# Feature columns in the order slot, sign, pair, head, and a new order list up to the second attention unit, in an adaLN block with linear attention

## The chip, the cores and the metric

The kernel runs on one core of a Trainium2 chip. The metric is the device time of one execution in microseconds; the time before is 408.78 us, the median of three runs (408.36 to 409.27).

## The reference

One transformer block on x of 2048 rows by 576, in bf16: conditioned layer norm, linear attention with 32 heads of width 18, conditioned layer norm, and a feed-forward layer of 4608 with ReLU.

```
mod = (silu(c) @ w_mod) in six rows: sa, ca, ga, sb, cb, gb
h   = layernorm(x) * (1 + ca) + sa
q, k, v = h @ wqkv, split in 32 heads of 18
pq, pk  = q @ w_phi[h], k @ w_phi[h]
phi(p)  = concat(softmax(p), softmax(-p))          # 36 features per head
kv  = phi(pk)^T @ v          z = sum of phi(pk) over the rows
o   = phi(pq) @ kv / (phi(pq) @ z + 1e-6)
x   = x + ga * (o @ wo)
h   = layernorm(x) * (1 + cb) + sb
out = x + gb * (relu(h @ w1) @ w2)
```

## The kernel before

**Tiling.** The 2048 rows are 16 tiles of 128 (a tile's index is `t`). The map `w_phi` and the norm's scale are folded into the key and query weights first (`F0`, `FA0`, `FB0`, `SC0` and others, L351 and L364), so one projection gives `pk` or `pq`. The first stage, to about 88 us, projects all keys and values and the first queries, makes the key features and sums the key-value product over all tiles (`KVa` to `KVc`, L636). Behind it the queries are taken in units of two tiles (unit 0 to 7): attention output, second norm, and the feed-forward layer of that unit.

**Features.** Heads are in 11 groups of `GH` = 3 (the last has 2). A head's 18 raw features are 9 slots `f` of 2 (pair `e`). A group's 108 columns (`DW`) in `phik` (keys) or `room` (queries) are ordered sign, slot, pair, head before: first 54 columns for the positive softmax, then 54 for the negative. Keys are evicted from PSUM into the first 54 columns and stay there as raw values; queries are evicted into `pq` on their own. In `softmax_parts`, `ext` builds the minimum and maximum over a head's features as a tree on VectorE (L474 to L479; steps `MN` and `MX` for the four tiles of a key block, `qMN` and `qMX` for a query unit). `less` writes minimum minus value into the negative half (L487, `LO`) and value minus maximum into the positive one (L489, `HI`). Then come the exponential on ScalarE (`EX`, L516), the sums, logarithm and exponential of the negative (`RC`, L539 and L541), and the scale on VectorE (`SC`, L547 for keys in one instruction, L551 for queries in two). Sums are made in one of two ways: on TensorE as nine matmuls with the identity, one a slot, added up in the PSUM tile `ps_sum` (`SU`, L523, and `SA`, which adds the pairs, L527), or on VectorE as one reduction a tile (`SD`, L534). Seven of the eight key pairs and the first query unit use TensorE; key tiles 12 and 13 and the other query units use VectorE.

**Order.** The kernel is recorded under a manual schedule: TensorE, VectorE, ScalarE and the DMA queue of SyncE each execute in the order in which the steps are written. Up to the second unit the steps stand in a string, `order`, one name a step; a name's letters choose the function, its numbers are arguments, and a last `.1` hands an eviction to the other engine: `KE`, `VE` and `QE` (evictions of keys, values and queries) go to ScalarE by default and to VectorE with it; `FA0`, `FB0` (fold evictions), `SC0`, `SC1` (scaling of weight rows) and `KVE` (key-value eviction) go to VectorE by default and to ScalarE with it. `K.t`, `V.t`, `Q.t` are projections of ten matmuls; their PSUM tiles come from a pool of three. `LS`, `RS`, `LX`, `LT` are the first norm and its transposing DMA. `qT` transposes the scaled query features by DMA into `ET`; `NU.j` and `NV.j` multiply them with the key-value product for unit 0 and unit 1 (L677). `HA.q` and `HB.q` are the two phases, by halves of TensorE's rows, of one of nine groups of the first feed-forward layer for unit 0 (L807), `RL` its ReLU, `Y` the second layer (L907). `LM`, `LW`, `W2`, `WOL` load weights, `RD` loads a gate row.

The sums on TensorE, and on VectorE:

```
for f in range(DH // 2):
    T_.matmul(ps, lhsT=ident[:], rhs=e[:, :, :, f * G2:(f + 1) * G2], start=(f == 0), stop=(f == DH // 2 - 1))
...
V.tensor_reduce(out=t["l", b][:, k * 22:(k + 1) * 22].rearrange("p (g s) h -> p g s h", s=2), op=ALU.add,
                axis=mybir.AxisListType.X, in_=E[:, j].rearrange("p g (s f h) -> p g s h f", s=2, h=GH))
```

Of the kernel before, what the change touches and what calls it, by code (L numbers as in the profile page):

```python
# [8 lines left out]
P = 128  # L9
# [34 lines left out]
def kernel(  # L44
# [23 lines left out]
    V, A_, G, T_ = nc.vector, nc.scalar, nc.gpsimd, nc.tensor  # L68
# [17 lines left out]
    def copy(eng, dst, src):  # L86
        if eng is A_:
            A_.activation(out=dst, in_=src, func=ACT.Copy)
        else:
            eng.tensor_copy(out=dst, in_=src)  # L90
# [6 lines left out]
    ident = const.tile([P, P], BF16, name="ident")  # L97
# [363 lines left out]
    PARTS = [(0, 5 * GF), (5 * GF, D - 5 * GF)]  # L461


    def softmax_parts(E, src, n, whole):

        ng = n * NG

        def slots(a, s=0):
            return a[:, :, :, s * GF:(s + 1) * GF].rearrange("p n g (f c) -> p (n g) f c", c=G2)

        def ext(op):
            src_, w = src.rearrange("p n g c -> p (n g) c"), 4 * G2
            a = work.tile([P, 4 * NG, w], BF16, name="tree", tag="tree", bufs=1)[:, 0:ng]
            V.tensor_tensor(out=a, in0=src_[:, :, 0:w], in1=src_[:, :, w:2 * w], op=op)  # L474
            for w in (2 * G2, G2):
                V.tensor_tensor(out=a[:, :, 0:w], in0=a[:, :, 0:w], in1=a[:, :, w:2 * w], op=op)  # L476
            V.tensor_tensor(out=a[:, :, 0:G2], in0=a[:, :, 0:G2], in1=src_[:, :, 8 * G2:9 * G2], op=op)
            r = work.tile([P, 4 * NG, 2, GH], BF16, name="root", tag="root", bufs=4)[:, 0:ng]
            V.tensor_tensor(out=r, in0=a[:, :, 0:GH].unsqueeze(2).to_broadcast([P, ng, 2, GH]),  # L479
                            in1=a[:, :, GH:G2].unsqueeze(2).to_broadcast([P, ng, 2, GH]), op=op)  # L480
            return r.rearrange("p a e h -> p a (e h)")

        def less(j, mn, mx):
            f = slots(src[:, j:j + 2])
            r = (mn if mx is None else mx)[:, j * NG:(j + 2) * NG].unsqueeze(2).to_broadcast([P, 2 * NG, DH // 2, G2])
            if mx is None:
                V.tensor_tensor(out=slots(E[:, j:j + 2], 1), in0=r, in1=f, op=ALU.subtract)  # L487
            else:
                V.tensor_tensor(out=slots(E[:, j:j + 2], 0), in0=f, in1=r, op=ALU.subtract)  # L489
# [28 lines left out]
        def sums_pe(j):  # L518

            ps = t["s", j] = aux_tile("ps_sum")[:, 0:2 * NG * 2 * G2].rearrange("p (a c) -> p a c", c=G2)  # L520
            e = E[:, j:j + 2].rearrange("p n g (s c) -> p (n g) s c", s=2)
            for f in range(DH // 2):
                T_.matmul(ps, lhsT=ident[:], rhs=e[:, :, :, f * G2:(f + 1) * G2], start=(f == 0), stop=(f == DH // 2 - 1))  # L523
# [6 lines left out]
        def sums(j):  # L530
            b, k = j // 2 * 2, j % 2
            if ("l", b) not in t:
                t["l", b] = work.tile([P, 4 * NG, GH], FP32, name="ln_s", tag="ln_s", bufs=2)
            V.tensor_reduce(out=t["l", b][:, k * 22:(k + 1) * 22].rearrange("p (g s) h -> p g s h", s=2), op=ALU.add,  # L534
                            axis=mybir.AxisListType.X, in_=E[:, j].rearrange("p g (s f h) -> p g s h f", s=2, h=GH))

        def recip(j):
            l = t["l", j]
# [2 lines left out]
            A_.activation(out=r[:], in_=l[:].unsqueeze(2).to_broadcast([P, 4 * NG, 2, GH]), func=ACT.Exp, scale=-1.0)  # L541

        def scale(j):
            r = t["r", j][:].rearrange("p a e h -> p a (e h)")
            if whole:
                e = E[:, j:j + 2].rearrange("p n g (s f c) -> p (n g s) f c", s=2, c=G2)
                V.tensor_tensor(out=e, in0=e, in1=r.unsqueeze(2).to_broadcast([P, 4 * NG, DH // 2, G2]), op=ALU.mult)  # L547
                return
            for s in range(2):
                e, q = slots(E[:, j:j + 2], s), r.rearrange("p (a s) c -> p a s c", s=2)[:, :, s]  # L550
                V.tensor_tensor(out=e, in0=e, in1=q.unsqueeze(2).to_broadcast([P, 2 * NG, DH // 2, G2]), op=ALU.mult)  # L551
# [25 lines left out]
    pss, pq_zero = {}, set()  # L577
# [5 lines left out]

    def features(dst, ps, eng):

        copy(eng, dst[:, 0:10, :].rearrange("p (a g) c -> p a g c", a=2),
             ps[:, :, 0:5 * GF].rearrange("p a (g c) -> p a g c", c=GF))
        copy(eng, dst[:, 10, :].rearrange("p (f h) -> p f h", h=GH)[:, :, 0:2],
             ps[:, 1, 5 * GF:5 * GF + 36].rearrange("p (f h) -> p f h", h=2))

    def keys_out(t, eng):
        features(phik_g(t // TPB)[:, t % TPB, :, 0:GF], pss["k", t], eng)

    def queries_out(t, eng):
# [24 lines left out]
    KVZ = const.tile([P, NG, GH * VH], BF16, name="KVZ")
# [361 lines left out]
    FB0.3.1 KE.6 SC0.3 KE.4 MN.1 RS.5 B0 BE0.1.1 V.7 LX.5 LM.0 BE0.0.1 LS.14 LM.1 HI.1 PM.3 Q.2 LT.10 VE.7 QE.2 RS.6
    Q.1 HI.0 K.8 QE.1 LT.11 Q.7 KE.8.1 MX.1 EX.0 QE.7 LS.15 Q.0 LX.6 Q.3 LO.3 QE.0 RS.7 SU.0 K.10 LT.9 QE.3.1 HI.3 K.11
    K.9 EX.1 KE.11 LO.2 WOL qMN.0 SA.0 LX.7 KE.10 KE.9 LT.12 SU.1 HI.2 EX.3 K.12 RW.1 RW.0 MN.2 SA.1 qMX.0 KE.12 LT.15
    SU.3 RWE.0.1 LT.14 K.15 RC.0 W1 qLO.0 K.14 RWE.1.1 LO.4 EX.2 KE.15 qHI.0 LT.13 Q.14 LO.5 MX.2 SA.3 KE.14 qEX.0
    QE.14 K.13 V.9 RC.1 HI.5 SU.2 HI.4 RC2.0 KE.13 MN.3 Q.4 LW.1.1 LO.7 VE.9 qEX.1 SA.2 V.8 EX.4 EX.5 QE.4.1 Q.13 MX.3
    V.6 VE.8 LO.6 SC.0 qSU.0 V.13 RC.2 SC.2 VE.6 qSA.0 RD.2 QE.13 Q.12 SU.5 RC.3 HI.6 VE.13 SC.3 qRC.0 V.10 EX.6 SU.4
    VE.10 SA.5 RC2.2 V.11 RC.5 QE.12 VE.11 qSC.0 V.12 SA.4 HI.7 EX.7 SC.1 SD.12 Q.8 V.15 RD.0 SD.13 SC.5 VE.12 VE.15
    SU.7 RC.4 SA.7 SC.4 RC.6 V.14 qT.0 QE.8 KVa LW.1.0 SC.6 VE.14 RC.7 KVb RC2.1 SC.7 LW.0.0 KVc Q.11 WS.1 KVE.0 LW.2.1
    KVE.1 LW.0.1 QE.11 WS.0 NU.1 Q.6 NU.0 NUE.1 OT.1 Q.10 NUE.0 qMN.1 OT.0 OTE.1 QE.6 OTE.0 MCE2 WO.1 QE.10 WOE.1 WO.0
    WOE.0 S2.1.1 R2.1 S2.0 R2.0 Q.15 X2.1 X2.0 Q.9 qLO.1 PN.1 PN.0 QE.15 PNE Q.5 QE.5 QE.9 qMX.1 qHI.1 qEX.3 HA.0 HA.1  # L990
    HA.2 qMN.2 HB.0 LW.2.0 P2 HB.1 qSD.3 qEX.2 HB.2 qSD.2 LW.3.1 qMX.2 LW.3.0 W2.0.0 W2.1.0 RL.0 W2.0.1 HA.3 RL.1 qRC.1
    RL.2 RD.1 HA.4 HB.3 HB.4 HA.5 RL.3 HA.6 W2.2.1 HB.5 RL.5 qSC.1 HB.6 W2.1.1 qT.1 NV.0 RL.6 Y.1.0.0 NVE.0 W2.2.0 OU.0
    NV.1 qHI.2 RL.4 Y.1.0.1 HA.7 qLO.2 NVE.1 qEX.4 qSD.4 qEX.5 HA.8 OU.1 WA.0 HB.7 WB.0 qSD.5 WPE.0 qRC.2 HB.8 RL.7
    WA.1 Y.1.1.0 qSC.2 WB.1 Y.1.1.1 WPE.1 RL.8 Y.1.0.2 S3.0 S3.1 Y.0.0.0 R3 X3 Y.1.1.2 YE.1.0 qT.2 NW.0 XT NWE.0
    Y.0.1.0 MD.0 Y.0.1.1 YE.1.1 Y.0.0.1 NW.1 OW.0 MD.4 Y.0.0.2 MD.3 NWE.1 Y.0.1.2 MD.2 YE.0.0 MD.1 OW.1 YE.0.1
    """
    for step in order.split():
        name, *at = step.split(".")
# [126 lines left out]
```

## Time and profile before

| | |
|---|---|
| median of 3 runs | 408.78 us (408.36 to 409.27) |
| profiled execution | 409.36 us, of which the span is 407.6 us |
| busy TensorE, VectorE, ScalarE | 399.2, 232.3, 181.7 us |
| granted TensorE clock | 1.00 |
| key-value product starts, its last matmul ends | 82.85, 87.92 us |
| numerator of the second unit (NV.0) starts | 114.51 us |

The span is one profiled execution from its first to its last instruction; what lies around it makes up the difference to that execution's own time. Times in rows of the trace count from the span's start. A row of the timeline has start, duration, engine, line and operation, then output and input, the shape, and how many instructions it groups; what stands in square brackets is idle time before it and who ended it. A row of the groups ends with busy time in us and the mean of one in ns.

### The profile page before, as it was taken

To read this page: it belongs to the slowest core of one execution; us is meant where nothing else is said; L and a number is where in the kernel's file an instruction comes from. 1 tells how busy PE (TensorE), PEld (TensorE's weight loads), DVE (VectorE), ACT (ScalarE), POOL (GpSimd) and SP (SyncE) were. 2 spreads that over 40 slices of the span, in tenths; PEclk is the share of its full clock that TensorE was granted. 3 is DMA by queue.
4 is the path that set the end of the run, shared out by engine and by line. 5 is a ranking of instruction groups with operands and counts; after the bars stand their busy time and mean duration, and the time that the engine had idled before them with its cause. 6 is when DMAs were issued, how large, how long until landed. Compare 5 with 4: busy or idle time off the path is not lost.

```text
span 407.6 us, 10671 instructions
## 1 busy us (share of the span) xinstructions
PE 399.2 (98%) x4572; PEld 298.3 (73%) x4572; DVE 232.3 (57%) x603; ACT 181.7 (45%) x337; POOL 19.4 (5%) x123
## 2 busy tenths in 40 slices
PE   6899999999999999999999999999999999999997
PEld 3777777797877888888888888655467774447776
DVE  6889999999766756685886579423202310000111
ACT  5899999938653065216422450144530005552000
POOL 8100000000000000000000000000000000000000
PEclk9999999999999999999999999999999999999999
DMA  8968950499973401423374216400040000000001
GB/s 235 290 109 214 210 128 17 75 262 370 279 180 72 95 3 34 89 60 58 70 98 83 38 21 129 71 2 1 2 66 16 14 31 2 0 2 2 14 18 29
DMA packets 71001, 35.53 MB, mean 87 GB/s; under 512 B 56673, under 2 KB 67434, under 8 KB 70954
## 3 DMA queue, kind: packets, MB, share of 16 engines
q1 hardware_dynamic: 70352, 34.83, 37.9%
q8 instruction: 36, 0.59, 0.6%
q10 hardware_dynamic: 602, 0.02, 0.1%
q14 instruction: 11, 0.09, 0.1%
HBM read 19.27 MB, written 2.37 MB: 53 GB/s over the span
## 4 chain that ended last, share of the span: by engine, by line
PE 89%; DVE 5%; DMA 2%; ACT 1%; issue 1%; SPq 0%; ACTq 0%
PE ps_y L907 35%; PE ps_h L807 31%; PE ps_v L457 5%; PE ps_k L457 5%; PE ps_wo L807 4%; PE ps_q L457 3%; PE ps_sum L523 2%; DMA kv_raw<-in_A_wqkv_dram 1%; PE ps_kv L636 1%; DMA ET<-room 1%; PE ps_num L677 1%; DVE ln_s L534 1%; DVE tree L476 1%; PE ps_bias L372 1%; DVE xn L239 0%
## 5 line engine op out<-in xcount | busy, mean ns | idle before, releaser
L907 PE MATMUL ps_y<-w_sb,H 128*128 128x288 bf16 x864 | 109.3, 286 | 0.0
L907 PEld LDWEIGHTS <-H 128*128 128x128 bf16 x864 | 82.9, 98 | 22.3 <-issue 2.0
L807 PE MATMUL ps_h<-hT2all,w1a 64*128 64x256 bf16 (+1 forms) x960 | 78.5, 305 | 0.0
L915 DVE TENSOR_TENSOR outt<-ps_y,row_gb 128x288 bf16<-128x288 f32 (+2 forms) x33 | 14.7, 445 | 103.0 <-PE ps_y L907 103.0
L807 PEld LDWEIGHTS <-w1a 64*128 64x128 bf16 x960 | 46.8, 94 | 22.0
L807 PE MATMUL ps_h<-hT2all,w1b 64*128 64x256 bf16 (+1 forms) x768 | 62.8, 305 | 0.0
L863 ACT ACTIVATE H<-ps_h 128x512 bf16<-128x512 f32 x36 | 21.5, 596 | 81.3 <-PE ps_h L807 81.3
L457 PEld LDWEIGHTS <-hT 128*128 128x128 bf16 x480 | 46.1, 97 | 12.2 <-issue 0.4
L890 ACT ACTIVATE H<-ps_h 128x1024 bf16<-128x1024 f32 x36 | 36.0, 1018 | 37.8 <-PE ps_h L807 37.8
L807 PEld LDWEIGHTS <-w1b 64*128 64x128 bf16 x768 | 37.4, 94 | 18.0
L724 DVE TENSOR_TENSOR x_sb<-x_sb,ps_wo 128x288 bf16<-128x288 bf16 x28 | 11.4, 450 | 42.4 <-PE ps_wo L807 42.4
L807 PE MATMUL ps_h<-hT2all,w1c 64*128 64x256 bf16 (+1 forms) x216 | 33.4, 305 | 0.0
L907 PE MATMUL ps_y<-w_sb,H1m 128*128 128x288 bf16 (+2 forms) x270 | 32.4, 273 | 0.0
L907 PEld LDWEIGHTS <-H1m 128*128 128x128 bf16 x270 | 24.5, 98 | 5.2
L516 ACT ACTIVATE room<-room 128x1188 bf16<-128x1188 bf16 x16 | 18.6, 1189 | 15.7 <-DVE room L489 13.9
L811 POOL MEMSET token<- 1x2 bf16 x86 | 8.2, 96 | 311.8 <-PE ps_h L807 291.6
L457 PE MATMUL ps_q<-wfold,hT 128*128 128x270 bf16 (+1 forms) x160 | 21.6, 285 | 0.0
L457 PE MATMUL ps_v<-wv_sb,hT 128*128 128x288 bf16 x160 | 21.4, 286 | 0.1
L457 PE MATMUL ps_k<-wfold,hT 128*128 128x270 bf16 (+1 forms) x160 | 21.2, 285 | 0.0
L227 DVE BATCH_NORM_STATS2 bst<-x_sb 128x6 f32<-128x288 bf16 x46 | 18.6, 445 | 1.5 <-DMA x_sb<-in_A_x_dram 1.5
L534 DVE TENSOR_REDUCE ln_s<-room 128x66 f32<-128x1188 bf16 x14 | 18.7, 1368 | 0.0
L864 ACT ACTIVATE H1m<-ps_h 128x512 bf16<-128x512 f32 x30 | 17.8, 592 | 0.0
(156 smaller groups left out, 442.9 us busy)
## 6 DMA issues: line engine op xcount, KB each, us to landing
w_sb<-in_B_w_dram SPq DMA_DIRECT2D x6, 864.0 KB, 12.4
out_dram<-outt SPq DMA_DIRECT2D x15, 144.0 KB, 1.9
w1b<-in_B_w_dram SPq DMA_DIRECT2D x2, 1024.0 KB
x_sb<-in_A_x_dram SPq DMA_DIRECT2D x3, 576.0 KB, 10.3
w1a<-in_B_w_dram SPq DMA_DIRECT2D x2, 768.0 KB
kv_raw<-in_A_wqkv_dram SPq DMA_DIRECT2D x4, 288.0 KB, 5.0
wma<-in_w_mod_dram SPq DMA_DIRECT2D x2, 576.0 KB
wmb<-in_w_mod_dram SPq DMA_DIRECT2D x2, 576.0 KB
```

Of the source, the lines that this page charges most:

```text
L227: V.bn_stats(out=st[:, half, :], in_=x_sb[:, t0 + j, half * 288:(half + 1) * 288])
L457: T_.matmul(ps[:, 0:cn], lhsT=lhs[:, ci, :], rhs=w[:, ci, cs:cs + cn], start=(ci == 0), stop=(ci == KC - 1))
L516: A_.activation(out=E[:, j:j + k], in_=E[:, j:j + k], func=ACT.Exp)
L534: V.tensor_reduce(out=t["l", b][:, k * 22:(k + 1) * 22].rearrange("p (g s) h -> p g s h", s=2), op=ALU.add, axis=mybir.AxisListType.X, in_ ...
L724: V.tensor_tensor(out=xs[:, cs:cs + cn], in0=xs[:, cs:cs + cn], in1=p[:, 0:cn], op=ALU.add)
L807: i = T_.matmul(ps, lhsT=l, rhs=r, start=(phase == 0 and k < 2), stop=(phase == 1 and k >= len(items) - 2))
L811: g = last[key] = G.memset(token[:], 0.0)
L863: A_.activation(out=p2t["H1"].rearrange("p (e j) n -> p e j n", e=2)[:, :, i, :], in_=f1[i][:, :, 0:U * P], func=ACT.Relu)
L864: A_.activation(out=h1_more(i), in_=f1[i][:, :, U * P:], func=ACT.Relu)
L890: A_.activation(out=p2t["H1"].rearrange("p (e j) n -> p e j n", e=2)[:, :, 2 * q:2 * q + 2], in_=f1[q][:].rearrange("p e (h n) -> p e h n" ...
L907: T_.matmul(ps[:, 0, 0:cn], lhsT=h, rhs=p2t["w2"][:, k, c], start=(k == 0), stop=(k == NJ - 1))
L915: V.tensor_tensor(out=o[:, c], in0=ps[:, 0, 0:cn], in1=rows["gb"][:, c], op=ALU.mult)
```

## The change

A group's columns are now ordered slot, sign, pair, head: for each slot the six positive features, then the six negative ones. The raw keys therefore lie in runs of 6 with a step of 12, the keys' evictions write 90 such runs (the last group 9x2x2), and trees and subtractions read and write them so; queries still come from `pq`, which is contiguous. The matmul of a slot reads its 12 columns of a group as one run. A tile's sums on VectorE become two reductions, one a sign, over two axes. The queries' scale becomes one instruction like the keys'. `pad_keys` clears all columns of the last group.

```diff
@@ softmax_parts
+        def signs(a):
+            return a.rearrange("p n g (f c) -> p (n g) f c", c=2 * G2)
+        def raw(j, k):
+            return signs(E[:, j:j + k])[:, :, :, 0:G2] if src is None else src[:, j:j + k].rearrange("p n g (f c) -> p (n g) f c", c=G2)
@@ ext
-            V.tensor_tensor(out=a, in0=src_[:, :, 0:w], in1=src_[:, :, w:2 * w], op=op)
+            V.tensor_tensor(out=a.rearrange("p a (f c) -> p a f c", c=G2), in0=x[:, :, 0:4], in1=x[:, :, 4:8], op=op)
@@ less
-                V.tensor_tensor(out=slots(E[:, j:j + 2], 1), in0=r, in1=f, op=ALU.subtract)
+                V.tensor_tensor(out=e[:, :, :, G2:], in0=r, in1=f, op=ALU.subtract)
@@ sums_pe
-            e = E[:, j:j + 2].rearrange("p n g (s c) -> p (n g) s c", s=2)
+            e = signs(E[:, j:j + 2])
-                T_.matmul(ps, lhsT=ident[:], rhs=e[:, :, :, f * G2:(f + 1) * G2], start=(f == 0), stop=(f == DH // 2 - 1))
+                T_.matmul(ps.rearrange("p (a s) c -> p a (s c)", s=2), lhsT=ident[:], rhs=e[:, :, f], start=(f == 0), stop=(f == DH // 2 - 1))
@@ sums
-            V.tensor_reduce(out=t["l", b][:, k * 22:(k + 1) * 22].rearrange("p (g s) h -> p g s h", s=2), op=ALU.add,
-                            axis=mybir.AxisListType.X, in_=E[:, j].rearrange("p g (s f h) -> p g s h f", s=2, h=GH))
+            l = t["l", b][:, k * 22:(k + 1) * 22].rearrange("p (g s) h -> p g s h", s=2)
+            e = E[:, j].rearrange("p g (f s e h) -> p g s h f e", s=2, e=2, h=GH)
+            for s in range(2):
+                V.tensor_reduce(out=l[:, :, s], op=ALU.add, axis=mybir.AxisListType.XY, in_=e[:, :, s])
@@ scale
-            for s in range(2):
-                e, q = slots(E[:, j:j + 2], s), r.rearrange("p (a s) c -> p a s c", s=2)[:, :, s]
-                V.tensor_tensor(out=e, in0=e, in1=q.unsqueeze(2).to_broadcast([P, 2 * NG, DH // 2, G2]), op=ALU.mult)
+            e, r = signs(E[:, j:j + 2]), t["r", j][:].rearrange("p (a s) e h -> p a (s e h)", s=2)
+            V.tensor_tensor(out=e, in0=e, in1=r.unsqueeze(2).to_broadcast([P, 2 * NG, DH // 2, 2 * G2]), op=ALU.mult)
@@ keys_out
-        features(phik_g(t // TPB)[:, t % TPB, :, 0:GF], pss["k", t], eng)
+        e = phik_g(t // TPB)[:, t % TPB].rearrange("p g (f c) -> p (g f) c", c=2 * G2)
+        features(e[:, :, 0:G2], pss["k", t], eng)
@@ order, its line around the product
-    SU.7 RC.4 SA.7 SC.4 RC.6 V.14 qT.0 QE.8 KVa LW.1.0 SC.6 VE.14 RC.7 KVb RC2.1 SC.7 LW.0.0 KVc Q.11 WS.1 KVE.0 LW.2.1
+    SU.7 SD.12 SC.3 VE.13 SA.7 RC.6 Q.10 VE.14 SC.6 RC.7 KVa SC.7 QE.10 KVb RD.0 KVc WS.0 KVE.0 KVE.1.1 Q.13 NU.1 WS.1
...
```

The string `order` is rewritten from its first value projection to the end of unit 0. Of the evictions, VectorE now has values 1, 2, 5 and 15 (before: 2), keys 0 (before: 0, 1, 8) and, ahead of the product, no query (before: 3 and 4); the fold evictions FA0.1, FB0.0 and FB0.3 and the scaling SC0.4 move to it, while SC1.1, SC0.2 and KVE.1 move to ScalarE. One more phase of the feed-forward layer, HA.7, stands ahead of NV.0. The tree of unit 2's maximum (qMX.2) stands behind NV.0, its first subtraction (qLO.2) ahead of the scale qSC.1; the load W2.0.1 is fifth of the second weights, not third, and RD.1 is earlier.

ScalarE, the last instructions up to the last exponential of the keys (`phik_449` is the last block of four tiles, `v` are evicted values), before:

```order
L541 ACTIVATE rsum<-ln_s 128x264
L516 ACTIVATE phik_449<-phik_449 128x2376
L88 ACTIVATE v_95<-ps_v 128x32x18
L539 ACTIVATE ln_s<-ln_s 128x132
L541 ACTIVATE rsum<-ln_s 128x264
L88 ACTIVATE room<-ps_q 128x540
L88 ACTIVATE room<-ps_q 128x18x2
L88 ACTIVATE v_95<-ps_v 128x32x18
L516 ACTIVATE phik_449<-phik_449 128x2376
```

And now:

```order
L88 ACTIVATE room<-ps_q 128x540
L88 ACTIVATE room<-ps_q 128x18x2
L544 ACTIVATE ln_s<-ln_s 128x132
L546 ACTIVATE rsum<-ln_s 128x264
L544 ACTIVATE ln_s<-ln_s 128x132
L546 ACTIVATE rsum<-ln_s 128x264
L88 ACTIVATE v_96<-ps_v 128x32x18
L88 ACTIVATE v_95<-ps_v 128x32x18
L519 ACTIVATE phik_449<-phik_449 128x2376
```

Two pairs of logarithm and reciprocal and two values now stand between the last query eviction and the exponential, where there was one value.

VectorE, from the last subtraction of the keys to the last scale, before:

```order
L489 TENSOR_TENSOR phik_449<-phik_449,root 128x22x54
L547 TENSOR_TENSOR phik_446<-phik_446,rsum 128x2376
L534 TENSOR_REDUCE ln_s<-phik_449 128x66 x2
L547 TENSOR_TENSOR phik_448<-phik_448,rsum 128x2376
L527 TENSOR_REDUCE ln_s<-ps_sum 128x132
L547 TENSOR_TENSOR phik_448<-phik_448,rsum 128x2376
L547 TENSOR_TENSOR phik_449<-phik_449,rsum 128x2376 x2
```

And now:

```order
L492 TENSOR_TENSOR phik_449<-phik_449,root 128x198x6
L550 TENSOR_TENSOR phik_448<-phik_448,rsum 128x2376 x2
L540 TENSOR_REDUCE ln_s<-phik_449 128x11x3 x4
L550 TENSOR_TENSOR phik_447<-phik_447,rsum 128x2376
L530 TENSOR_REDUCE ln_s<-ps_sum 128x132
L550 TENSOR_TENSOR phik_449<-phik_449,rsum 128x2376 x2
```

Five scales stand there as before, but two come ahead of the reductions, of which there are four and not two.

TensorE at the numerator of the second unit (`ET` the transposed queries, `w1b` and `w1c` parts of the first feed-forward weights), before:

```order
L807 LDWEIGHTS w1b_1938
L807 MATMUL ps_h_2095<-hT2all_172,w1b_1938 128x256
L677 LDWEIGHTS ET_2154
L677 MATMUL ps_num_2157<-KVZ_174,ET_2154 128x57
L677 LDWEIGHTS ET_2154
```

And now, at the same count of instructions from the start:

```order
L806 LDWEIGHTS w1b_1840
L806 MATMUL ps_h_2074<-hT2all_172,w1b_1840 128x256
L806 LDWEIGHTS w1c_1192
L806 MATMUL ps_h_2153<-hT2all_172,w1c_1192 128x256
L806 LDWEIGHTS w1c_1192
```

The numerator has moved behind the twenty matmuls of HA.7, which begin here.

More of the change, by code (lines that the diff above doesn't have):

```diff
@@ L483, in less @@
         def less(j, mn, mx):
-            f = slots(src[:, j:j + 2])
+            f, e = raw(j, 2), signs(E[:, j:j + 2])
             r = (mn if mx is None else mx)[:, j * NG:(j + 2) * NG].unsqueeze(2).to_broadcast([P, 2 * NG, DH // 2, G2])
             if mx is None:
-                V.tensor_tensor(out=slots(E[:, j:j + 2], 1), in0=r, in1=f, op=ALU.subtract)
+                V.tensor_tensor(out=e[:, :, :, G2:], in0=r, in1=f, op=ALU.subtract)
             else:
-                V.tensor_tensor(out=slots(E[:, j:j + 2], 0), in0=f, in1=r, op=ALU.subtract)
+                V.tensor_tensor(out=e[:, :, :, 0:G2], in0=f, in1=r, op=ALU.subtract)
         t = {}
@@ L598, in queries_out @@
             G.memset(pq[b][:, :, NG - 1, :], 0.0)
-        features(pq[b][:, j], pss["q", t], eng)
+        features(pq[b][:, j].rearrange("p g (f c) -> p (g f) c", c=G2), pss["q", t], eng)
     def values_out(t, eng):
@@ L981 @@
[L981 to L985, printed above, removed]
@@ new lines @@
+    VE.0 K.2 LS.7 K.1 RS.2 LS.12 VE.2.1 LX.2 LQ.2 LQ.3 K.0 KE.2 LS.10 F0.4 RS.3 LT.4 LX.3 KE.1 KE.0.1 K.3 F0.0 FB0.4
+    LT.6 FA0.4 LS.11 LT.5 F0.1 LS.9 FB0.1 LT.7 KE.3 LS.13 FA0.1 V.4 FB0.0 MN.0 VE.4 FA0.0.1 K.6 LM.1 RS.6 SC0.4 F0.2
+    RS.4 LO.0 FB0.2.1 K.5 FA0.2.1 KE.6 V.7 LM.2 LX.4 MX.0 KE.5 SC0.0 SC0.2.1 F0.3 VE.7 PM.3 K.4 FA0.3.1 RS.5 FB0.3 KE.4
+    V.5 LS.14 HI.0 VE.5.1 K.7 KE.7 LT.8 PM.2 B0 SC0.1 LM.0 LX.5 LT.11 BE0.1.1 BE0.0.1 RW.1 SC0.3 LO.1 MX.1 LS.15 Q.0
+    HI.1 MN.1 RWE.1.1 RS.7 LX.6 Q.2 QE.2 QE.0 K.8 LO.3 Q.1 LO.2 LT.9 KE.8 K.9 Q.3 LT.10 EX.1 QE.1 EX.0 LX.7 SU.1 qMX.0
@@ new lines @@
+    HI.3 K.10 KE.9 qMN.0 KE.10 SU.0 HI.2 K.11 RW.0 LT.15 LT.14 QE.3 qLO.0 RC2.0 LT.13 EX.3 SA.0 SA.1 Q.7 RWE.0.1 KE.11
+    EX.2 RD.2 QE.7 K.15 Q.4 LT.12 SU.2 qHI.0 MN.2 K.13 KE.15 RC.0 MX.2 RC.1 QE.4 LO.5 LO.4 V.11 KE.13 VE.11 qEX.1 WOL
+    qEX.0 RD.1 K.14 SA.2 K.12 KE.12 SC.0 V.9 SU.3 KE.14 W1 RC.2 SC.1 LW.1.0 qSU.0 Q.14 HI.4 V.15 HI.5 RC2.2 VE.9 MN.3
+    qSA.0 LO.6 SA.3 EX.4 MX.3 SU.4 VE.15.1 EX.5 QE.14 Q.8 qRC.0 SU.5 RC2.1 V.10 HI.6 qSC.0 SC.2 QE.8 LW.0.1 Q.12 V.8
+    RC.3 SA.5 EX.6 SA.4 VE.10 qT.0 QE.12 RC.4 V.12 V.6 RC.5 VE.12 VE.8 V.14 LO.7 HI.7 SC.4 SC.5 V.13 EX.7 VE.6 SD.13
```

47 lines of the change are left out of this document (17 added, 30 removed).

## The prediction

> **What bounds the kernel now.** I read the first part of the page, then the busy time of the first stage, then the order of work at the two places where the order list changes what waits. The page, each engine's busy time and share of the span:
>
> ```profile
> PE 399.2 (98%) x4572; PEld 298.3 (73%) x4572; DVE 232.3 (57%) x603; ACT 181.7 (45%) x337; POOL 19.4 (5%) x123
> ```
>
> TensorE has work for 98% of the span, so only two things shorten the run: matmuls that take less time, and waits of TensorE that go. But the average hides the first stage, up to the key-value product. Its busy time in stretches, columns TensorE matmul, weight load, VectorE, ScalarE, GpSimd:
>
> ```profile
> 17.00:80.00 63.00, 62.93 (x565) 48.85 (x561) 59.80 (x139) 59.97 (x129) 2.56 (x11) 1.00 0.63 121
> 17.00:87.00 70.00, 69.93 (x732) 55.20 (x728) 66.80 (x145) 64.15 (x139) 2.56 (x11) 1.00 0.67 134
> ```
>
> There three engines are full: VectorE 66.8 of 70 us, ScalarE 59.97 of the 63 us up to the last exponential of the keys (3.03 us idle). Whoever makes TensorE faster here meets the other two. The end of that stage, in order of start:
>
> ```profile
> 77.78 2.19 ACT L516 ACTIVATE phik<-phik 128x2376 bf16<-128x2376 bf16 x1
> 80.43 1.35 PE L523 MATMUL ps_sum<-phik,ident 128*128 128x264 bf16 x9
> 82.85 5.23 PE L636 MATMUL ps_kv<-v,phik 128*128 128x57 bf16 x176
> 82.87 4.00 DVE L547 TENSOR_TENSOR phik<-phik,rsum 128x2376 bf16<-128x2376 bf16 x3
> 87.92 0.87 PE L457 MATMUL ps_q<-wfold,hT 128*128 128x270 bf16 x6
> ```
>
> The last exponential (EX.7) ends at 79.97; its sums on TensorE (SU.7) start at 80.43, so they have 0.46 us in hand. The last scale ends at 86.87; its two tiles are the last of sixteen in the product, which reaches them at about 82.85 + 14/16 x 5.07 = 87.29: 0.42 us in hand.
>
> **Sums on TensorE.** They stay 72 matmuls of 264 columns in 8 groups; what changes is that their operand is read in 22 runs of 24 bytes, not 44 of 12. Starts before, first V projections of 288 contiguous columns and what follows, then a group for keys and what follows, then the query group with rows that begin at its second, third, fourth and fifth matmul:
>
> ```profile
> 17.79 5.08 PE L457 MATMUL ps_v<-wv_sb,hT 128*128 128x288 bf16 x40
> 22.70 0.51 PE L457 MATMUL ps_k<-wfold,hT 128*128 128x270 bf16 x3
> 46.09 1.35 PE L523 MATMUL ps_sum<-phik,ident 128*128 128x264 bf16 x9
> 47.27 0.39 PE L457 MATMUL ps_k<-wfold,hT 128*128 128x270 bf16 x2
> 68.22 1.41 PE L523 MATMUL ps_sum<-room,ident 128*128 128x264 bf16 x9
> 68.36 0.47 PE L523 MATMUL ps_sum<-room,ident 128*128 128x264 bf16 x2
> 68.51 0.43 PE L523 MATMUL ps_sum<-room,ident 128*128 128x264 bf16 x2
> 68.66 0.42 PE L523 MATMUL ps_sum<-room,ident 128*128 128x264 bf16 x2
> 68.77 0.46 PE L523 MATMUL ps_sum<-room,ident 128*128 128x264 bf16 x2
> 69.47 0.29 PE L457 MATMUL ps_v<-wv_sb,hT 128*128 128x288 bf16 x1
> ```
>
> Contiguous: (22.70 - 17.79)/40 = 122.8 ns for 288 columns, so 112.5 for 264. Keys: (47.27 - 46.09)/9 = 131 ns. Query group: 1.25/9 = 139, and the matmuls of one group differ, 140, 150, 150 and 110 ns, though only the place of their runs differs. With the old layout's addresses, a slot's 12-byte runs touch 66 or 88 stretches of 16 bytes in the slow ones and 44 in the quick ones; the new runs start at a multiple of 8 bytes and touch 44 always. I take 114 to 116 ns: 63 x 16 + 9 x 24 = 1.2 us of TensorE time. Bounds: nothing (the cost is not of the runs) and 63 x 18.5 + 9 x 26.5 = 1.4. The Trainium skill, "Advanced Engine Details and Errata", section "SBUF Cachelines", says that lines are 16 bytes and that a line wants at least two hits; that fits the 110 against 150 ns above. Its "TensorE: Matmul & The Clock Gate", section "Wait — 56ns, not 53.3ns?", gives start to start as columns by 2.4 GHz plus about 2.5 ns, whatever the layout: by that the groups would already run at 112.5 and this term would be nothing; the rows disagree.
>
> All of it lies before the product, so SU.7 could start 1.1 us earlier, at 79.3, if its exponential were there. It had 0.46 us in hand, so ScalarE decides.
>
> **ScalarE up to the last exponential.** Counting both lists up to it, it gets 2 key evictions, 2 query evictions, 1 pair of logarithm and reciprocal and 1 scaling of a weight row more; 3 value evictions and 3 fold evictions fewer.
>
> ```profile
> L88 ACT ACTIVATE v<-ps_v 128x576 bf16<-128x576 f32 x15 | 9.6, 647 | 0.2
> L88 ACT ACTIVATE phik<-ps_k 128x540 bf16<-128x540 f32 x13 | 7.9, 616 | 0.0
> L88 ACT ACTIVATE phik<-ps_k 128x36 bf16<-128x36 f32 x13 | 2.7, 208 | 0.0
> L88 ACT ACTIVATE room<-ps_fold 128x432 bf16<-128x432 f32 x5 | 2.6, 530 | 0.7 <-PE ps_fold L351 0.7
> L88 ACT ACTIVATE room<-ps_fold 128x144 bf16<-128x144 f32 x6 | 1.6, 293 | 0.0
> L539 ACT ACTIVATE ln_s<-ln_s 128x132 f32<-128x132 f32 x16 | 5.0, 314 | 25.5 <-DVE ln_s L534 24.9 <-DVE ln_s L527 0.6
> L541 ACT ACTIVATE rsum<-ln_s 128x264 bf16<-128x264 f32 x16 | 6.8, 423 | 0.8 <-DVE phik L547 0.3
> ```
>
> 4 x (0.616 + 0.208) + 0.737 + about 0.5 - 3 x 0.647 - 0.530 - 2 x 0.293 = +1.5 us, against 3.03 us idle. With the idle unchanged the exponential would end at 81.5, with none at 78.4. Walking the new list by hand (each instruction starts at the later of its input and its predecessor, durations from such rows) I come to 80.0 to 80.1, with half of the idle used up. TensorE meanwhile waits for evictions and folds in six places, 0.04 to 0.2 us each, about as much as before. So SU.7 starts at 80.05, 0.38 earlier than before; its own group is 0.15 shorter, and one projection follows it as before (now a query's, not the last value's). The product starts and ends 0.5 us earlier, near 87.4. **Term one: -0.5 us**; 0.7 of the 1.2 us turns into waits. That the keys' evictions write 90 runs of 6 rather than 10 of 54 I cost at nothing: in these rows an eviction's price goes with its elements, 616 ns for 540 and 530 for 432; bound 0.1 us for each of 15, which would move the exponential by up to 1 us.
>
> **VectorE up to the last scale.** Its rows:
>
> ```profile
> L90 DVE CAST v<-ps_v 128x576 bf16<-128x576 f32 x1 | 0.8, 750 | 0.0
> L90 DVE CAST phik<-ps_k 128x540 bf16<-128x540 f32 x3 | 2.1, 711 | 0.1
> L90 DVE CAST phik<-ps_k 128x36 bf16<-128x36 f32 x3 | 0.6, 188 | 0.0
> L534 DVE TENSOR_REDUCE ln_s<-phik 128x66 f32<-128x1188 bf16 x2 | 2.7, 1380 | 0.0
> L527 DVE TENSOR_REDUCE ln_s<-ps_sum 128x132 f32<-128x264 f32 x8 | 3.4, 424 | 0.0
> L551 DVE TENSOR_TENSOR room<-room,rsum 128x1188 bf16<-128x1188 bf16 x16 | 11.7, 772 | 0.3
> L547 DVE TENSOR_TENSOR phik<-phik,rsum 128x2376 bf16<-128x2376 bf16 x8 | 10.8, 1386 | 0.0
> L489 DVE TENSOR_TENSOR phik<-phik,root 128x1188 bf16<-128x1188 bf16 x8 | 6.0, 770 | 0.0
> L474 DVE TENSOR_TENSOR tree<-phik 128x1056 bf16<-128x1056 bf16 x8 | 5.6, 700 | 0.1
> ```
>
> - Evictions: +3 values, -2 keys, -2 queries: 2.25 - 1.80 - 1.80 = -1.3; three fold evictions (one large, two small, at the ScalarE rows or a little more) +1.2, a scaling of a weight row away, -0.3.
> - Sums as two instructions: from 264 to 1188 elements a reduction grows from 424 to 1380 ns, 1.03 ns an element plus 0.15 fixed, so two of 594 cost 1.53 and not 1.38: +0.15 each, +0.3 for the two of the keys. The 14 for queries lie in stages where VectorE has slack.
> - Query scale as one instruction: 1.386 for 2 x 0.772: -0.16.
> - First step of the trees and both subtractions, strided now: nothing. The subtractions already work on 6-element runs by a broadcast operand at 0.65 ns an element (770 for 1188), and the first tree step, whole rows, has 0.66 (700 for 1056): contiguous or not, the same. Bound: one element at a time as the reduction, 1.03 + fixed.
>
> Sum -0.3 to about +0.15, since neighbours overlap. The last scale then ends near 86.6, and the product, 0.5 earlier, needs it at 86.8. It just fits; this is the next to be late.
>
> **Behind the product.** Half the key-value eviction goes to ScalarE as five small activations, about 5 x 0.21 = 1.05 us (the 36-element row), beside a query projection of 1.23 us: hidden, and TensorE needs it only for the ninth to eleventh group. The gap at NV.0, the numerator of the second unit, before:
>
> ```profile
> 109.94 3.95 SPq L664 DMA_TRANSPOSE ET<-room  x2
> 110.19 0.27 PE L807 MATMUL ps_h<-hT2all,w1c 64*128 64x256 bf16 x2
> 111.28 0.27 PE L807 MATMUL ps_h<-hT2all,w1c 64*128 64x256 bf16 x2
> 111.94 2.35 PE L807 MATMUL ps_h<-hT2all,w1b 64*128 64x256 bf16 x40
> 114.51 0.41 PE L677 MATMUL ps_num<-KVZ,ET 108*128 108x57 bf16 x8 [0.23 <-DMA ET<-room]
> ```
>
> Twenty matmuls of a first phase take 111.28 - 110.19 = 1.09 us, so the 40 end their turn at 111.94 + 2.18 = 114.12, and the numerator starts at 114.51: 0.39 us lost to the transposes. With one more phase ahead of it (HA.7), it is due at 114.12 + 1.09 - 0.5 = 114.7, when the transposes have landed even if they are no earlier. **Term two: -0.4 us.** Nothing else takes the place: the phase is only moved, and the fifth load of the second weights, now W2.0.1, has more than 2 us in hand as I follow the queue.
>
> Sum: -0.9 us. The profiled execution is 409.36 (span 407.6), so 408.46; the median of the runs is 0.58 lower than that execution: 407.9.
>
> **Rivals.**
> 1. The whole saving comes through: ScalarE finishes the exponential by 79.3, and some early waits (0.04 to 0.2 each) go as well. For it: 3.03 us of idle against 1.5 of new work. Against: the idle is made by what ScalarE waits for. -1.2 - 0.4 - 0.2 = -1.8: 407.0.
> 2. ScalarE eats everything: the exponential 0.4 us later than I walked, at 80.4 or after. For it: +1.5 us of work on an engine that is 95% full. -0.4 or nothing in all: 408.4 to 408.8.
> 3. The sums don't get quicker (the change doesn't do what it says): 131 ns stays. SU.7 then has as much in hand as before, and only NV.0 gains: 408.4. The clock page's rule above comes to the same time by the other road, that they are quick already.
> 4. The other side: the strided key features cost the trees their rate. Eight first tree steps at 1.03 ns an element, 1.24 for 0.70 us, are +4.3 us on VectorE, which has 0.2 in hand before the last scale; the product, 0.5 early, then ends 3.6 late, and term two takes 0.4 off: 412.0. It decides from 0.05 us a step. Against it the rows of 770 and 700 ns. The Trainium skill, "VectorE: DVE Perf Modes", section "Mode 2×_1P — pack two bf16 into one 32-bit read", asks for step ±1 and 4-byte alignment; runs of 6 keep both inside a run, and here only a run can show whether the jump between runs counts.
> 5. An early wait of the new order that I mis-walked (a value eviction on VectorE holding one of the three PSUM buffers) costs 1 us or more before the product: 409 to 410.
>
> **How the numbers follow.** A difference under 0.2%, 0.82 us, is about what a measurement of this kernel can't tell from none. Chances: my forecast 0.42 (407.4 to 408.4), rival 1 0.22, rival 2 0.12, rival 3 0.10, rival 4 0.07, rival 5 0.07. The forecast lies just past the bound (407.96), so 0.25 of its 0.42 count as faster, with 0.21 of rival 1 and 0.03 of rivals 2 and 3: 0.49. Same: 0.17 + 0.01 + 0.19 = 0.37. Slower: rivals 4 and 5, 0.14. The range leaves out rival 4 and the tails: from 406.3 (rival 1 with the sums' upper bound and the waits before the product, some 0.6, all gone: 408.78 - 1.4 - 0.4 - 0.6) to 409.6 (rival 5's middle).
>
> **What would show it.** In the new trace: groups of nine sums matmuls that start 1.03 to 1.05 us before what follows, not 1.18; SU.7 directly behind an exponential that ends near 80.0, with a TensorE wait of some 0.7 us there; the product's end near 87.4; no wait ahead of the numerator near 114.7; reductions of 0.76 us in pairs; first tree steps at 0.70. Wrong would be made by an exponential that ends before 79.4 or after 80.5, by tree steps over 0.75, by sums that still take 131 ns, or by a new wait between 20 and 60 us.

## The result and the profile after

The changed kernel takes 412.66 us (median of 6 runs, 411.0 to 413.38) against 408.93 for the kernel before: 1.0086 times, 95% interval 1.0072 to 1.0100. It is slower by 3.7 us, where 0.9 us faster was forecast. The profiled execution has a span of 410.9 us, 3.3 more than before, and these waits of TensorE (work, line, who was waited for; total us, times, longest):

```profile
PE ps_kv L635 <- issue: 1.8, 1, 1.8
PE ps_wo L806 <- DMA oT<-o_tm: 0.8, 1, 0.8
PE ps_h L806 <- POOL token L810: 0.8, 3, 0.3
```

None of the three is in the profile before. The first stage's end, in order of start, answers to the rows from 77.78 to 87.92 before:

```profile
77.23 2.19 ACT L519 ACTIVATE phik<-phik 128x2376 bf16<-128x2376 bf16 x1
79.63 1.20 PE L526 MATMUL ps_sum<-phik,ident 128*128 128x264 bf16 x9
80.67 1.39 PE L457 MATMUL ps_q<-wfold,hT 128*128 128x270 bf16 x10
81.90 3.63 PE L635 MATMUL ps_kv<-v,phik 128*128 128x57 bf16 x121
83.49 2.72 DVE L550 TENSOR_TENSOR phik<-phik,rsum 128x2376 bf16<-128x2376 bf16 x2
87.29 1.76 PE L635 MATMUL ps_kv<-v,phik 128*128 128x57 bf16 x55 [1.76 <-issue]
88.90 1.39 PE L457 MATMUL ps_q<-wfold,hT 128*128 128x270 bf16 x10
```

The sums groups are quick as forecast: nine matmuls in 80.67 - 79.63 = 1.04 us, 115 ns each. The product starts at 81.90, 0.95 us earlier than before. Then, after 121 of its 176 matmuls, TensorE stands still for 1.8 us with "issue" as the reason: the profile names nothing that it waits for. Behind the product, rows of TensorE and ScalarE:

```profile
89.76 0.99 ACT L647 ACTIVATE KVZ<-ps_kv,m_fh 108x38 bf16<-108x38 f32 x5 [4.75 <-DVE KVZ L649]
90.12 0.86 PE L676 MATMUL ps_num<-KVZ,ET 108*128 108x57 bf16 x11
90.83 1.39 PE L457 MATMUL ps_q<-wfold,hT 128*128 128x270 bf16 x10
101.70 0.28 PE L806 MATMUL ps_h<-hT2all,w1c 64*128 64x256 bf16 x2
103.18 1.05 PE L806 MATMUL ps_h<-hT2all,w1a 64*128 64x256 bf16 x16 [0.21 <-POOL token L810]
111.49 1.05 PE L806 MATMUL ps_h<-hT2all,w1a 64*128 64x256 bf16 x16 [0.27 <-POOL token L810]
114.99 1.92 PE L806 MATMUL ps_h<-hT2all,w1b 64*128 64x256 bf16 x32 [0.27 <-POOL token L810]
117.94 0.40 PE L676 MATMUL ps_num<-KVZ,ET 108*128 108x57 bf16 x8
124.66 0.79 PE L806 MATMUL ps_wo<-wo_sb,oT 64*128 64x288 bf16 x10 [0.84 <-DMA oT<-o_tm]
```

Starts against those of the kernel before give the sum. The idle time in brackets understates a loss, because the last matmul's modelled end covers some of it; the losses here are from start to start, less what the same step takes where nothing waits (0.03 us inside the product, 0.11 between two phases or ahead of the output projection, 0.20 ahead of the numerator).

| place | us |
|---|---|
| up to the product's start, 81.90 for 82.85 | -0.95 |
| hole in the product (1.92 from start to start; product to next 88.90 - 81.90 for 5.07) | +1.93 |
| first numerator, 0.71 us to the next projection for 0.32 | +0.39 |
| three second phases behind their own first (0.37, 0.43, 0.43) | +1.23 |
| numerator of the second unit waits no more | -0.30 |
| output projection of the second unit waits | +1.00 |
| sum, against 3.3 between the spans | +3.30 |

VectorE and ScalarE, the forms whose price was forecast:

```profile
L477 DVE TENSOR_TENSOR tree<-phik 128x1056 bf16<-128x1056 bf16 x8 | 5.6, 701 | 0.0
L540 DVE TENSOR_REDUCE ln_s<-phik 128x33 f32<-128x594 bf16 x4 | 3.2, 870 | 0.0
L88 ACT ACTIVATE phik<-ps_k 128x540 bf16<-128x540 f32 x15 | 9.5, 646 | 0.2 <-PE ps_k L457 0.2
L88 ACT ACTIVATE phik<-ps_k 128x36 bf16<-128x36 f32 x15 | 3.8, 252 | 0.0
```

### The profile page after: what moved, and what is told of

The parts are those of the page before. It is cut to its first block, busy times and chain, and to the rows that moved or that the text cites. A ratio compares the mean times of both kernels' runs of the same rounds, so it can differ in the third digit from the quotient of the medians.

```text
span 410.9 us, 10673 instructions
## 1 busy us (share of the span) xinstructions
PE 400.3 (97%) x4572; PEld 298.5 (73%) x4572; DVE 236.4 (58%) x608; ACT 182.8 (44%) x343; POOL 20.2 (5%) x123
## 4 chain that ended last, share of the span: by engine, by line
PE 92%; DMA 2%; ACT 2%; DVE 2%; issue 1%; SPq 0%; POOL 0%; DVEq 0%; ACTq 0%; POOLq 0%
PE ps_y L906 34%; PE ps_h L806 34%; PE ps_q L457 4%; PE ps_wo L806 4%; PE ps_k L457 4%; PE ps_v L457 4%; PE ps_sum L526 2%; PE ps_kv L635 1%; DMA kv_raw<-in_A_wqkv_dram 1%; DMA oT<-o_tm 1%; PE ps_num L676 1%; PE ps_wT L341 1%; PE ps_fold L351 1%; PE ps_wo L457 1%; PE ps_bias L372 1%
## 5 line engine op out<-in xcount | busy, mean ns | idle before, releaser
L540 DVE TENSOR_REDUCE ln_s<-room 128x33 f32<-128x594 bf16 x28 | 22.3, 854 | 0.9 <-ACT room L519 0.9
L544 ACT ACTIVATE ln_s<-ln_s 128x132 f32<-128x132 f32 x16 | 5.1, 321 | 28.6 <-DVE ln_s L540 28.2
```

Source lines behind the costliest of these rows:

```text
L540: V.tensor_reduce(out=l[:, :, s], op=ALU.add, axis=mybir.AxisListType.XY, in_=e[:, :, s])
```

## Experiments

**What the hole is.** The DMA queues of the profile before have a line with 36 packets, 0.59 MB: 16 KB a packet, and about 64 bytes for each of TensorE's 9144 matmuls and weight loads:

```profile
q8 instruction: 36, 0.59, 0.6%
```

Around 150 us three of these packets come 7.1 us apart (142.07, 149.16, 156.26), and exactly 256 TensorE instructions start between one and the next, when the 38 semaphore and drain instructions in its trace are counted too. So this is taken to be TensorE's fetch of its own program, a block of 256 at a time. From here on matmuls and weight loads alone are counted, in order of start. Before, the sixth packet came at 81.26, when TensorE was at instruction 1449. After, TensorE passed 1449 at 80.33, but the packet came at 84.68, at instruction 1667, and TensorE stood still behind 1714. From 80.0 to 84.6 the changed kernel's queues (packets, MB, busy share of the 16 DMA engines) have no such packet, and the engines are full with data; the next 1.3 us have it:

```profile
q1 hardware_dynamic: 1029, 1.32, 106.2%
...
q1 hardware_dynamic: 415, 0.43, 99.7%
q8 instruction: 1, 0.02, 5.4%
```

The new list issues three loads of the first feed-forward weights, 1.8 MB, from 77.35 on (the first row); the kernel before issues three of the same sizes at 79.73, 83.62 and 84.80:

```profile
77.35 1.68 SPq L760 DMA_DIRECT2D w1a<-in_B_w_dram  x3
...
79.73 0.77 SPq L761 DMA_DIRECT2D w1a<-in_B_w_dram  x1
83.62 0.58 SPq L761 DMA_DIRECT2D w1a<-in_B_w_dram  x1
84.80 0.59 SPq L761 DMA_DIRECT2D w1a<-in_B_w_dram  x1
```

Two kernels tested this reading. *late_w1* moves those loads in SyncE's queue:

```diff
- qMN.1 LW.0.0 LW.2.1 WO.1 ... S2.1.1 LW.1.1 MCE2 ... QE.6 HA.0 QE.9 LW.2.0 HB.0 RL.0 LW.3.0 HA.1
+ qMN.1 LW.0.0 WO.1 ... S2.1.1 MCE2 ... QE.6 LW.3.0 LW.2.1 LW.1.1 LW.2.0 HA.0 QE.9 HB.0 RL.0 HA.1
```

> The changed kernel with three loads of the first feed-forward weights (1.8 MB, issued at 77.35 to 79.0 us there) moved in SyncE's queue behind the load that waits for the key-value product. Theory 1 (TensorE ran out of instructions at 85.5 us: its next 16 KB of instructions were fetched at 84.68, about 4 us after they were due, behind those loads): the fetch starts within 1 us of 80.5, the product runs through, and the time falls by about 1.8 us, from 412.6 to 410.8. Rival (the 122nd matmul of the product waits for a scale or an eviction that the profile does not name): the hole of 1.8 us stays, 412.6.

Measured: 410.55 us, 1.0034 of before (1.0022 to 1.0045). The fetch comes at 80.84, and the product runs through:

```profile
82.27 5.23 PE L635 MATMUL ps_kv<-v,phik 128*128 128x57 bf16 x176
87.35 0.87 PE L457 MATMUL ps_q<-wfold,hT 128*128 128x270 bf16 x6
```

2.1 us are back by moving loads that TensorE does not use until 100 us. *shift10* leaves every load and wait alone:

```diff
     fill(1)
+    for _ in range(10):
+        T_.matmul(ps[:, 0:16], lhsT=zeros[:, 0:P], rhs=zeros[:, 0:16], start=True, stop=True)
```

> The changed kernel with ten matmuls of 16 columns more at the start, where TensorE is idle, and nothing else: 20 instructions more ahead of everything. Theory 1 (the hole is at the end of the instructions that TensorE holds): the hole moves ten matmuls to the front, from behind the 121st matmul of the product to behind the 111th, and stays of the order of 1 to 2 us; the time stays within 1 us of 412.6. Rival (a wait for data): it stays behind the 121st.

Measured: 410.55 us, 1.0024 (1.0012 to 1.0037). The hole neither stayed nor moved, it vanished: TensorE passed 1449 at 79.39, and the fetch came 1.2 us behind that, at 80.55, and not 4.3. Why it waited less is not shown. The expectation was wrong in that, but a wait for data is ruled out, since nothing on which the product depends was touched and VectorE's last scales even start later there (83.61 for 83.49). The kernel before must then be exposed too, which *before_s31* showed by accident; it was made for the last wait below and has 62 instructions more and nothing else:

```diff
- Z.3 WT.0 LS.3
+ Z.3 WT.0 ZS.31 LS.3      # ZS: 31 matmuls of 16 columns
```

> The kernel before with 31 matmuls of 16 columns more at the start, where TensorE waits for a load, and nothing else. There the fetch at 120.14 us lies behind the transposes issued at 116.74; 62 instructions more put it near 118.4, among their packets. Theory 1 (a fetch among the packets holds them up): TensorE now waits ahead of the second unit's output projection, 0.4 to 0.8 us, and the kernel is slower by that, 409.4. Rival (the fetch does not touch the transposes): no wait there, within 0.2 us of before.

Measured: 412.18 us, 1.0070 (1.0057 to 1.0084), slower than either theory said, and not at that place. The seventh fetch, at 90.99 in the kernel before, comes at 93.05, and TensorE stands still between the first numerator's matmuls behind instruction 1968, which it reached at 90.86:

```profile
PE ps_num L682 <- issue: 4.7, 1, 4.7
```

(4.7 us in the profiled execution, the slowest of its six, 415.91; the others lie at 411.7 to 412.9.) From 80.0 to 93.0 its queues have no instruction packet either, with the engines at 104.1%. With the semaphore and drain instructions the two places, 1714 and 1968, are numbers 1729 and 1985: 256 apart, one block. Three more kernels below, order_only, phases and kve_dve, stop at the first of them (at 1713 in the last two, whose traces have one instruction less), and all five holes end 1.2 to 1.6 us after the late packet is through (84.68 + 1.13, then 87.29 in the changed kernel).

Part of the 415.91 is not the hole itself. Behind it the granted TensorE clock was 0.5 from 94.12 to 100.95 us (it is the number after the five engines):

```profile
94.20:100.90 6.70, 5.17 (x29) 3.66 (x30) 3.04 (x12) 2.63 (x6) 0.00 (x0) 0.50 1.06 375
```

The profile of *phases* below has the same behind its hole, from 88.06 to 91.48; that of the changed kernel has not, but that kernel's two slowest executions, 413.04 and 413.38, have a mean clock of 0.996 and the other four 1.000. That the hole brings the clock down is likely and not tested.

So 62 instructions in idle time cost 3 us: they bring TensorE to the end of the instructions that it holds 3.4 us earlier (90.86 for 94.26), and the next ones, held up in the weight loads, come 2.1 us later. The kernel before is close to the same: with its packet at 90.99, 1.15 us of transfer and 1.2 to 1.6 us until TensorE goes on, it would have had its instructions at 93.4 to 93.7, and it reached number 1968 at 94.26.

**The other three places.** *phases* keeps each second phase away from its own first:

```diff
- HA.0 QE.9 LW.2.0 HB.0 RL.0 LW.3.0 HA.1 W2.0.0 ... HA.4 HB.4 RL.3 HA.5 RL.4 ... HA.6 HB.6 HB.5
+ HA.0 QE.9 LW.2.0 HA.1 HB.0 RL.0 LW.3.0 W2.0.0 ... HA.4 RL.3 HA.5 HB.4 RL.4 ... HA.6 HB.5 HB.6
```

> The changed kernel with no second phase directly behind the first phase of the same group: HA.1 ahead of HB.0, HA.5 ahead of HB.4, HB.5 ahead of HB.6. Theory 1 (the three waits for GpSimd's token cost TensorE 0.37 to 0.43 us each, since the token is set only when the first phase is done): the three waits go and the time falls by 1.2 us, to 411.4. Rival (the next thing is late then, the transposes ahead of the numerator of the second unit): the time falls by less than 0.5 us.

Measured: 411.79 us, 1.0065 (1.0047 to 1.0084), 0.9 below the changed kernel. No wait for the token is left among TensorE's waits, and from the first phase to the numerator it is 118.31 - 103.16 = 15.15 us for 16.24, so 1.09 of the 1.23 are back; what is missing went into one new wait for a PSUM tile, 0.19. *kve_dve* gives the second part of the key-value eviction back to VectorE:

```diff
- KVE.0 KVE.1.1 Q.13
+ KVE.0 KVE.1 Q.13
```

> The changed kernel with the second part of the key-value eviction back on VectorE as in the kernel before. Theory 1 (ScalarE's five small activations start only when VectorE's part is done, and end 0.4 us after TensorE needs them): TensorE's waits inside the first numerator, 0.39 us, go and the time falls by 0.3 to 0.4 us. Rival (VectorE is then late with the scaling of the output weights): no change.

Measured: 412.2 us, 1.0081 (1.0061 to 1.0102): 0.4 less by the medians, 0.2 by the ratios to before, and the intervals overlap; its profiled hole is shorter too, 1.2 us for 1.8. So the time doesn't show it, but the trace does: the first numerator takes 0.32 us again:

```profile
89.91 0.47 PE L676 MATMUL ps_num<-KVZ,ET 108*128 108x57 bf16 x11
90.23 1.39 PE L457 MATMUL ps_q<-wfold,hT 128*128 128x270 bf16 x10
```

**List or layout.** *order_only* is the kernel before with the new list in place of its own, *layout_only* the changed kernel with the old list; their diffs are the two parts of the change.

> The old column order with the new order list. Theory 1 (the list makes the loss): the phase waits, the wait inside the first numerator and that ahead of the output projection are all there, 2.5 us together, and the time is 411 to 413, by whether the instruction fetch is late here too. Rival (the layout makes part of the loss): below 410.5.

> The new column order, sums and scale with the order list of the kernel before. Theory 1 (the layout alone gains, the list loses it): sums groups start 1.04 us before what follows and not 1.18, the product starts 0.4 to 0.9 us earlier, and the time is 408.4, 0.5 us below before. Rival (two reductions for one and the dearer key evictions, 0.36 us a pair and 0.07 us an eviction, use that up on VectorE and ScalarE): within 0.3 us of before or slower.

Measured: order_only 412.75 us, 1.0092 (1.0077 to 1.0106), as slow as the changed kernel with the sums still at the old price, and with the same waits (its hole is 0.9, as its TensorE reaches that place 1.1 us later). layout_only 409.46 us, 1.0010 (1.0001 to 1.0018). So the list makes the loss, and the layout alone gains nothing, as its rival had it. It starts the product at 81.95, 0.9 earlier, and VectorE takes it back:

```profile
PE ps_kv L635 <- DVE phik L550: 0.5, 1, 0.5
PE ps_v L457 <- DVE room L90: 0.4, 1, 0.4
```

The last scale is late by 0.63 from start to start, a query eviction by 0.57. *layout_qe4* takes that eviction off VectorE:

```diff
- EX.4 EX.5 QE.4.1 Q.13
+ EX.4 QE.4 EX.5 Q.13
```

> The new columns with the order list of the kernel before, but the eviction of the queries of tile 4 on ScalarE, between two exponentials, and not on VectorE. Theory 1 (with the new columns VectorE is the bound of the first stage: its dearer sums make it late by 0.57 us for a value projection at 66 us and by 0.66 us for the last scale, while TensorE's sums are 1.2 us cheaper): 0.8 us less on VectorE takes most of both waits away, the product ends near 87.0 and the time falls from 409.5 to 408.5, 0.4 below the kernel before. Rival (ScalarE's exponentials, then up to 1 us later, take VectorE's place as the bound): 409.2 or more.

Measured: 408.79 us, 0.9991 (0.9982 to 1.0000): the fastest of all, 0.4 below before, no clear gain. The product ends at 86.99, as expected, and the first phase starts 0.93 us before its old time. The numerator of the second unit then starts 0.97 us after the matmul ahead of it, for 0.50 before (0.20 where nothing waits), since its transposes land only 0.5 us earlier: half of the gain is given back there.

```profile
PE ps_num L676 <- DMA ET<-room: 0.7, 1, 0.7
```

**Repairs together.** *repaired* is late_w1, phases and kve_dve in one.

> The changed kernel with three repairs in one: the three loads behind the key-value product, no second phase directly behind its own first, the second part of the key-value eviction on VectorE. Theory 1 (the causes are separate and add): 412.6 - 2.1 - 1.1 - 0.4 = 409.0, with the wait of about 0.8 us ahead of the second unit's output projection still there. Rival (they share one critical chain, so that mending one uncovers the next): 409.8 or more.

Measured: 409.87 us, 1.0018 (1.0009 to 1.0026). The separate gains, 2.1, 0.9 and 0.4, sum to 3.4; 2.8 came, and the time is the rival's and not the 409.0 of the theory. Where the rest went was not followed. The remaining wait is that of the output projection:

```profile
PE ps_wo L806 <- DMA oT<-o_tm: 0.9, 1, 0.9
```

Two kernels went for it. *repaired_w2* moves the last second-layer load ahead of the transposes, which stand earlier in the list too, *repaired_s20* adds 20 small matmuls to repaired as above.

```diff
- W2.0.1 HA.6 ... HA.7 qT.1 W2.2.1 NV.0
+ W2.0.1 W2.2.1 HA.6 qT.1 ... HA.7 NV.0
```

> The same three repairs, and the last load of the second feed-forward weights ahead of the second unit's query transposes in SyncE's queue instead of behind them. Theory 1 (the transposes of the second unit's attention output wait behind that load): TensorE's wait of about 0.8 us ahead of the output projection goes, 408.2, below the kernel before. Rival (the wait is that of the transposes alone, after a cover that is 0.2 us shorter): it stays at 0.5 us or more, and the query transposes may now be late instead: 409.0 or more.

> The kernel with the three repairs and 20 matmuls of 16 columns more at the start, where TensorE waits for a load. In the other kernels with the new list the fetch of TensorE's instructions that is due about row 2700 (118.5 us in the repaired kernel, 1.7 us long) lies in the transposes of the second unit's attention output (issued at 117.4), and their last packets come 1 to 1.5 us after the bulk. Theory 1 (those packets wait behind the fetch on one DMA engine): the fetch now comes at about 116.2, ahead of the transposes, TensorE's wait ahead of the output projection falls from 1.1 us to 0.4 or less, and the time from 409.9 to 409.0. Rival (the transposes take 4.3 us from issue to use by themselves): the wait stays above 0.8 us and the time at 409.9.

Measured: repaired_w2 411.06 us, 1.0052 (1.0034 to 1.0070), as the rival had it. The load is out of the way, the wait stays at 0.6, and the query transposes are now behind the load, 1.5 us late for the numerator. repaired_s20 409.36 us, 0.9998 (0.9988 to 1.0009), but the wait ahead of the output projection is still 0.7, and the fetch came at 118.65, as late as in repaired (118.48), though TensorE passed instruction 2701, where it comes there, at 116.77 already. So this did not test what it was for. *best* is repaired_s20 with the phases in the old pattern, three, three, two, two.

```diff
- HA.0 QE.9 HA.1 HB.0 ... HA.2 ... HA.3 ... HB.2 HB.1 ... HB.3 ... HA.4 ... HA.5 HB.4 ...
+ HA.0 QE.9 HA.1 HA.2 ... HB.0 ... HB.1 ... HB.2 ... HA.3 ... HA.4 HB.3 ... HB.4 ... HA.5 ...
```

> The kernel with the three repairs and 20 small matmuls, and the phases of the feed-forward layer in the pattern of the kernel before (three first phases, three second ones, then two and two), with HA.7 ahead of the numerator. Theory 1: the remaining wait of 0.2 us for a free PSUM tile among the phases goes as well, 408.7, below the kernel before by 0.2 us. Rival (the second unit's scale is later, since its exponentials now stand ahead of the first ReLU): the query transposes come late for the numerator, a wait of 0.3 us or more there, 409.2 or more.

Measured: 409.35 us, 1.0004 (0.9995 to 1.0013), no better than repaired_s20: the wait for a PSUM tile did not go but grew to 0.5 us, start to start, because the first ReLU now stands behind the exponentials. The numerator has no wait, so the rival's reason is not the one.

**What stays open.** From the issue of the transposes that feed the output projection to that projection it takes 4.16 to 4.59 us in all ten kernels with the new list and 3.72 to 3.99 in the four with the old one, which waited 0.1 us for it at most. The new list also has 0.2 us less work between the numerator and that projection, a second phase (0.87) where the old one has a first (1.09). In the changed kernel a fetch of TensorE's instructions (121.41 to 122.96) lies among the packets; most are through by 122.25, the last at 123.78. In the kernel before no fetch lies there and the last packet is through at 119.30. In before_s31 one does, and the last packet comes 1.0 us after the bulk, but that kernel waits 0.1 us only. That the fetch holds them up is likely and not shown.

## Why the prediction was wrong, step by step

- **Sums on TensorE, 114 to 116 ns:** right, 115 (rows at 79.63 and 80.67), so the runs were the cost.
- **Term one, product 0.5 us earlier:** the start came 0.95 earlier (in the repaired kernels 0.6 to 0.9). The walk put the last exponential's end at 80.0; it came at 79.42, because ScalarE's idle time up to 80 us fell from 3.03 to 1.25 (the row below) and not to 1.5. Up to that exponential ScalarE had 1.2 us more work (61.17 us for 59.94), not 1.5. So the term was undersized; the product's end was forecast at 87.4 and came at 88.9 for a reason that no step held.

```profile
17.00:80.00 63.00, 62.61 (x565) 49.03 (x562) 60.64 (x134) 61.75 (x134) 3.35 (x11) 1.00 0.68 136
```

- **"The product starts and ends 0.5 us earlier, near 87.4":** this is the step that failed first and cost most, 1.93 us. It lets the product run through once it has begun. Of the loads the prediction followed one, the fifth of the second weights, and only to its own user; for that one it was right, TensorE has no wait for it. The three loads of the first weights, which the new list issues ahead of the product, are not in it, nor is what else goes through the DMA engines, though the page had the line of instruction packets, and though the kernel before had only some 0.6 to 0.9 us in hand there itself. The runs showed a fetch of instructions 4.3 us late behind these loads. The Trainium skill, "Runtime: NRT & Kernel Launch", section "Instruction fetch mechanics", says that a block of 256 instructions is fetched while the one before runs and that this is mostly hidden. The packets agree with the block; the hole of 1.8 us is a case where the fetch is not hidden.
- **"Nothing else takes the place: the phase is only moved":** the count of phases was compared, not their neighbours. A second phase waits for the token that GpSimd sets once its own first phase is done; with that directly ahead, nothing covers it, 1.23 us.
- **Key-value eviction "hidden":** costed at 1.05 us beside a projection of 1.23. It starts only when VectorE's part is done (the row at 89.76 waited for VectorE's write to the same tile), so the two go one after the other. 0.39 us.
- **Term two, -0.4 at the numerator:** the wait went as said, but it was 0.30: from the matmul ahead to the numerator it took 0.50, and 0.20 of that is there without a wait. And 1.00 came at the output projection: 0.2 of it because a second phase now covers the transposes where the first phase HA.7 did, the rest because from their issue it took 4.50 us and not 3.72, for a cause that stays open.
- **Terms that were mis-sized off the path:** half-size reductions 854 to 870 ns, not 766; the keys' evictions 646 and 252 ns, not 616 and 208, inside the bound of 0.1 for each. Of these 0.07 us only 0.04 are the short runs: order_only, with the old columns and the new list, has 632 and 222. Neither makes TensorE wait more than 0.2 us in the changed kernel; in layout_only the reductions are part of what VectorE lacks.
- **Rival 4 gave 412.0,** close to what came, by another mechanism: the strided tree steps take 701 ns for 700. Nearness of a number shows nothing of its reason. Rival 5, an early wait, held the right kind of cause at the wrong place.

## What to carry to other kernels

Before moving loads earlier, look up the queue that carries the instructions: where TensorE issues a weight load and a short matmul each 29 ns it uses up 256 instructions in 3.7 us, and one late packet behind data loads stops it with no culprit in the table of waits but "issue". Compare the neighbours of a moved step and not the counts: a step that covered a wait is missed where it stood, and two that depend on each other need something between them. And a number of instructions more or less anywhere ahead can move a fetch into the loads, so a change of under 1% is not read without the packets' times.

## What was not expected of the hardware

- A fetch of 16 KB waited 4.3 us while data loads filled the DMA engines (80.33 to 84.68), and in five kernels the engine went on only 1.2 to 1.6 us after the transfer.
- Behind a hole of 1.9 us in one execution and of 4.9 us in another, from start to start, the granted clock was 0.5 for 3.4 and 6.8 us.
- 62 instructions added in idle time made the kernel before slower by 0.7%.
- The price of an identity matmul of 264 columns in runs of 12 bytes is 131 to 139 ns, in runs of 24 bytes 115.
- A reduction over two axes with an inner run of 2 took 854 to 870 ns for 594 elements, 1.45 ns each, where one axis of 18 took 1380 for 1188, 1.16 each.
